# V of the memory rows turned by transposing DMA through DRAM in place of TensorE transposes

## The chip, the cores and the metric

The kernel runs on one core of a Trainium2 chip. The metric is device time in microseconds (us). A kernel's runs mostly lie within 0.2% of each other. The names in the profile: PE is TensorE's matmuls, PEld its weight loads, DVE is VectorE, ACT ScalarE, POOL GpSimd, and SP the engine whose queue issues most of the DMAs (SPq in the views).

## The reference, cut to what matters

Two independent heads are concatenated. Head A is a state-space layer; its last stage is a matmul that shares TensorE with the start of head B. Head B is attention over segments of 32 tokens, each with 8 memory rows in front; the memory is the output of the segment before:

```python
for s in range(n_seg):                       # 64 segments of 32 tokens, 32 heads of 128
    h = jnp.concatenate([mem, xs], axis=1)   # 8 memory rows + 32 tokens
    q, k, v = (jnp.einsum('btd,dhe->bhte', h, W) for W in (Wq, Wk, Wv))
    ...                                      # masked softmax
    o = jnp.einsum('bhqk,bhke->bhqe', p, v)
    o = jnp.einsum('bhte,hed->btd', o, Wo)
    mem = o[:, :M, :].copy()
```

The kernel guesses all memory rows at once (73 distinct rows), computes everything in parallel, and checks the guess at the end. The change concerns only V of those 73 rows.

## The kernel before: the parts that matter

`v_mem(hb)` computes V of the 73 memory rows for one block of four heads. There are eight blocks (`hb`). The product leaves PE with the head dimension on the partitions, so it must be turned before it goes to DRAM (`b_vx`, `b_vt`), from where the attention loads it together with V of the tokens.

```python
def v_mem(self, hb, w=None):
    p = k.ps("P")
    ...                                            # 32 matmuls: V transposed, 4 heads x 73 columns
    vm = self.vmp.tile([128, 4, NM], BF16, name="b_vm", bufs=1)
    k.copy("v", vm[:], ...p...)                    # DVE: PSUM to SBUF
    yield
    pt = k.ps("P", (128, 1024), BF16)
    for h in range(4):
        k.PE.transpose(pt[0:NM, h * 128:(h + 1) * 128], vm[:, h, :], k.ident[:])
    st = self.next_st()                            # one of two staging buffers b_vst, in turn
    k.copy("v", st[0:NM, 0, :, 0:E], ...pt...)     # DVE: PSUM to SBUF
    sv = st[:, 0, :, :].rearrange("p h e -> p (h e)")
    k.SP.dma_start(self.vx[hb][64:64 + NMX, :], sv[0:NMX, :])
    k.SP.dma_start(self.vt[hb][:], sv[NMX:NM, :])
    yield
```

Each row of V carries a column of ones (for the softmax sum); in the staging buffer these columns were set once, at the start. Blocks 0 and 1 are turned during the last output tiles of head A (`i` 26 to 29 of 32). Blocks 2 to 7 are turned inside the attention loop, two head pairs ahead of their use.

Right after blocks 0 and 1 the attention starts with its first load of V:

```python
def load_v(self, hp):
    ...
    if hp < 2:      # zeros for the partitions that V does not fill: 128 - GW = 29 of them
        z = self.vx[0][T + 32:T + 32 + 128 - GW, 0:2 * EW].unsqueeze(1).to_broadcast([128 - GW, NG, 2 * EW])
        k.tc.keep_in_program_order(k.SP.dma_start(vt[GW:128, :, :], z))
    ...             # then 96 partitions from b_vx, 3 from b_vt
```

Of the kernel before, what the change touches and what calls it, by code (L numbers as in the profile page):

```python
# [9 lines left out]
BF16 = mybir.dt.bfloat16  # L10
# [16 lines left out]
HB = 8; HP = 16  # L27
# [7 lines left out]
NMX = 7  # L35
NM = NTL + NMX
# [3 lines left out]
EW = E + 8  # L40
# [13 lines left out]
class Pinned:  # L54


    def __init__(self, k, name, eng):
        self.k, self.name, self.eng = k, name, eng
# [278 lines left out]
class PartB:  # L337
    def __init__(self, k, x, mem0, Wq, Wk, Wv, Wo, out):
        self.k = k
        self.x, self.mem0, self.out = x, mem0, out  # L340
        self.Wf = [w.rearrange("(c p) h e -> p c (h e)", p=128) for w in (Wq, Wk, Wv)]
        self.Wo = Wo.rearrange("h e d -> e h d")
        self.vx = [k.drp.tile([NSLOT, 4 * EW], BF16, name=f"b_vx{i}") for i in range(HB)]
        self.vt = [k.drp.tile([NTL, 4 * EW], BF16, name=f"b_vt{i}") for i in range(HB)]
        self.on = [k.drp.tile([T, 1024], BF16, name=f"b_on{i}") for i in range(4)]
        self.tn = [k.drp.tile([NR, 1024], BF16, name=f"b_tn{i}") for i in range(4)]
        c = k.cst
        self.m0T = c.tile([128, KC, M], BF16, name="b_m0T")
        self.gx = c.tile([128, KC, NM], BF16, name="b_gx")
        self.vmp = c  # L350
        self.xbar = c.tile([128, KC, NSEG], BF16, name="b_xbar")
        self.ogT = c.tile([128, H, NSEG], BF16, name="b_ogT")
        self.accE = c.tile([128, HP * NU], FP32, name="b_accE")
        self.accR = c.tile([128, HP * 2 * NG], FP32, name="b_accR")
        self.flag = c.tile([1, 1], I32, name="b_flag")
# [184 lines left out]
    def v_mem(self, hb, w=None):  # L540
        k = self.k
        w = w or self.load_wv(hb)
        p = k.ps("P")
        for h in range(4):
            for c in range(KC):
                k.PE.matmul(p[:, h * NM:(h + 1) * NM], w[:, c, h * 128:(h + 1) * 128], self.memT[:, c, :], start=(c == 0), stop=(c == KC - 1))
        vm = self.vmp.tile([128, 4, NM], BF16, name="b_vm", bufs=1)
        k.copy("v", vm[:], p[:, 0:4 * NM].rearrange("p (h n) -> p h n", h=4))
        yield
        pt = k.ps("P", (128, 1024), BF16)  # L550
        for h in range(4):
            k.PE.transpose(pt[0:NM, h * 128:(h + 1) * 128], vm[:, h, :], k.ident[:])
        st = self.next_st()
        k.copy("v", st[0:NM, 0, :, 0:E], pt[0:NM, 0:512].rearrange("p (h e) -> p h e", h=4))
        sv = st[:, 0, :, :].rearrange("p h e -> p (h e)")
        k.SP.dma_start(self.vx[hb][64:64 + NMX, :], sv[0:NMX, :])
        k.SP.dma_start(self.vt[hb][:], sv[NMX:NM, :])
        yield


# [414 lines left out]
def kernel_main(tc, A_x, A_Lre, A_Lim, A_Bre, A_Bim, A_Cre, A_Cim, A_logdt, A_Dskip, B_x, B_mem0, B_Wq, B_Wk, B_Wv, B_Wo, out,  # L975
                force=False, dbg=None):
    with ExitStack() as ctx:
        k = K(tc, ctx)
# [3 lines left out]
        b = PartB(k, B_x, B_mem0, B_Wq, B_Wk, B_Wv, B_Wo, out)  # L982

        def pool(name, side, bufs=2):
            return tc.tile_pool(name=name, bufs=bufs, side=side, reuse_waits="tile")
# [8 lines left out]
        with pool("p1x", "right") as p1x, pool("p1", "right", 1) as p1:  # L994
# [10 lines left out]
            wv = {0: w0, 1: b.load_wv(1)}  # L1005
# [17 lines left out]
            for kind, pc, q in order[1:]:  # L1023
# [3 lines left out]
                if kind == "v":  # L1027
                    b.v_x(pc, q, wv[pc])
                    if q == 3:
                        if pc >= 3:  # L1030
                            b.og(pc, wv[pc])
                        n = (pc + 2) if pc + 2 < PC else (2, 0)[pc + 2 - PC]
# [3 lines left out]
                n = 4 * pc + q  # L1036
# [27 lines left out]
        with pool("p2h", "right") as p2h, pool("p2", "right") as p2:  # L1064
            a.s2_tiles(p2h, p2)
            g = b.guess(p2)
            s2 = a.stage2()
            b.wog = []
            a.load_h(1, nc.scalar)
            for i, _ in enumerate(s2):  # L1070
                if i in (1, 4, 7):
                    n = (2, 0, 1)[(i - 1) // 3]
                    b.og(n, wv[n], "O")
                    if n == 2:
                        wv[1] = b.load_wv(1)
                if i in (3, 7, 11, 15):
                    b.load_wog((3, 7, 11, 15).index(i), p2)
                if i in (9, 11, 13, 15, 17, 19, 21, 22):
                    next(g)
                if i == 20:  # L1080
                    b.load_wqk(0)
                if i == 23:
                    for _ in g:
                        pass
                if i in (26, 28):
                    vm = b.v_mem((i - 26) // 2, wv[(i - 26) // 2])
                if 26 <= i < 30:
                    next(vm)


# [15 lines left out]
        for n, (hp, u) in enumerate(at):  # L1106
            if n == 12:
                k.SP.dma_start(wo0[:], b.Wo[:, :, 0:512])
            if hp % 2 == 0 and 2 < hp + 2 < HP:
                if u == 4:  # L1110
                    vm = b.v_mem(hp // 2 + 1)
                if u in (4, 6):
                    next(vm)
            if hp == 13 and u in (3, 6, 9):
                b.load_o_early(u // 3 - 1)
            want = min(18 * HP, LEAD + (n + 1) * 18 // 11)
            while done < want:
                next(pr)
                done += 1
            if done == 18 * HP:  # L1120
                if first is None:
                    xs.close()
                    b.p4a = ctx.enter_context(pool("p4a", "left", 1))
                    wo1 = b.p4a.tile([128, H, 512], BF16, name="wo1")
                    b.wo = (wo0, wo1)
                    b.load_o_early(3)
                    for h in range(0, H, 16):
                        k.SP.dma_start(wo1[:, h:h + 16, :], b.Wo[:, h:h + 16, 512:D])
                    first = b.outproj_first()
                next(first)  # L1130
# [30 lines left out]
@with_exitstack  # L1161
def kernel(
    ctx: ExitStack,
    tc: tile.TileContext,
    A_x: bass.AP,
    A_Lambda_re: bass.AP,
    A_Lambda_im: bass.AP,
    A_B_re: bass.AP,
    A_B_im: bass.AP,
    A_C_re: bass.AP,  # L1170
    A_C_im: bass.AP,
    A_log_dt: bass.AP,
    A_Dskip: bass.AP,
    B_x: bass.AP,
    B_mem0: bass.AP,
    B_Wq: bass.AP,
    B_Wk: bass.AP,
    B_Wv: bass.AP,
    B_Wo: bass.AP,
    B_seg_len: bass.AP,  # L1180
    out: bass.AP,
):
    assert int(B_seg_len) == SEG
    kernel_main(tc, A_x, A_Lambda_re, A_Lambda_im, A_B_re, A_B_im, A_C_re, A_C_im, A_log_dt, A_Dskip,
                B_x, B_mem0, B_Wq, B_Wk, B_Wv, B_Wo, out)
# [35 lines left out]
```

## Time and profile before

| kernel before | |
|---|---|
| time | 1247.24 us, median of 4 runs (1247.18 to 1247.70) |
| span of the profiled run | 1245.6 us |
| PE busy | 1234.4 us (99%) |

Three lines of the page of the kernel before (busy time, share of the span, number of instructions; then the chain of waits by engine):

```profile
span 1245.6 us, 20120 instructions
PE 1234.4 (99%) x8270; PEld 662.3 (53%) x8342; DVE 668.0 (54%) x1250; ACT 263.5 (21%) x631; POOL 275.8 (22%) x407
PE 98%; DMA 1%; issue 0%; ACT 0%; POOL 0%; DVE 0%; SPq 0%; ACTq 0%
```

PE is the bottleneck from end to end. Its own list of waits, whole (who waited for whom: us in total, times, longest), holds 2.4 us:

```profile
PE psR L64 <- DVE hpb L105: 1.3, 1, 1.3
PE psO L64 <- POOL b_m L644: 0.9, 3, 0.4
PE psP L64 <- ACT b_xe L89: 0.2, 1, 0.2
```

So whatever makes PE wait lengthens the kernel. PE's timeline of the kernel before shows the four transposes of block 0 between two runs of head A's matmuls, and later the first use of `b_v`. Columns: start, length, engine, line, operation, operands, count.

```profile
455.76 0.39 PE L64 MATMUL psP<-ident,b_vm 128*73 128x128 bf16 x4
455.99 3.62 PE L64 MATMUL psP<-t,a_hl 128*128 128x512 bf16 x16
...
492.05 0.34 PE L64 MATMUL psS<-b_q,b_k 128*128 128x99 bf16 x4
492.23 0.50 PE L64 MATMUL psO<-b_v,b_m 128*128 128x129 bf16 x6
```

Records of matmuls overlap, so the length of a row overstates its cost; from start to next start the four transposes hold PE for 0.23 us. SP's timeline of the kernel before around the same place (the length is how long SP is in the issue, not how long the data takes):

```profile
457.01 0.30 SPq L64 DMA_DIRECT2D b_vx<-b_vst  x1
457.36 0.30 SPq L64 DMA_DIRECT2D b_vt<-b_vst  x1
460.71 0.41 SPq L64 DMA_DIRECT2D b_wv<-in_B_Wv_dram  x1
465.22 0.27 SPq L64 DMA_DIRECT2D b_vx<-b_vst  x1
465.54 0.30 SPq L64 DMA_DIRECT2D b_vt<-b_vst  x1
465.93 0.25 SPq L64 DMA_DIRECT2D b_v<-b_vt  x1
466.23 16.11 SPq L64 DMA_DIRECT2D b_v<-b_vx  x2
```

The last line is the 29-partition zero fill and the main load. SP sits in them for 16 us, and PE uses the result at 492.23 without a wait. Narrower windows of the same view show the two apart:

```profile
466.23 0.32 SPq L64 DMA_DIRECT2D b_v<-b_vx  x1
466.60 15.74 SPq L64 DMA_DIRECT2D b_v<-b_vx  x1
```

By the semaphore updates in the trace, the last part of the main load landed at 491.56 us, 0.7 us before its use.

### The profile page before, as it was taken

The page shows a single profiled execution, that of the slowest core. Times are in us where ns is not written, and L with a number is a line of the kernel's source. Part 1 is how long each engine was busy: PE and PEld are TensorE (multiplying, and loading weights), DVE is VectorE, ACT ScalarE, POOL GpSimd, SP SyncE. Part 2 cuts the span into 40 slices and gives each one's busy share as a digit, 9 for nine tenths or more (in the row PEclk, how much of TensorE's full clock was granted, in tenths as well). Part 3 has the DMA queues.
Part 4 walks back from the last instruction along what each step waited for, and adds up shares of the span by engine and source line. Part 5 has one row for each costly group of instructions (what it writes and reads, how often), then busy time and mean ns, then how long its engine had stood idle before and what let it go on. Part 6 is the DMA issues. An engine that isn't in the chain of part 4 may idle for free.

```text
span 1245.6 us, 20120 instructions
## 1 busy us (share of the span) xinstructions
PE 1234.4 (99%) x8270; PEld 662.3 (53%) x8342; DVE 668.0 (54%) x1250; ACT 263.5 (21%) x631; POOL 275.8 (22%) x407
## 2 busy tenths in 40 slices
PE   9999999999999999999999999999999999999998
PEld 5444444444455555556666656555665554446444
DVE  4688899998711124666666666666666641001000
ACT  5344444443310000211112111111211110000000
POOL 4111331212332321322222222222222220000000
PEclk9999999999999999999999999999999999999999
DMA  9965444554898834664454544545473289407000
GB/s 245 272 192 148 131 132 128 144 156 107 241 323 247 251 116 95 192 167 123 95 144 108 144 108 114 138 92 133 96 155 95 61 223 220 110 18 153 17 17 27
DMA packets 316022, 176.83 MB, mean 142 GB/s; under 512 B 138650, under 2 KB 301326, under 8 KB 315926
## 3 DMA queue, kind: packets, MB, share of 16 engines
q1 hardware_dynamic: 293830, 147.95, 48.1%
q10 hardware_dynamic: 21072, 24.38, 5.9%
q0 software_dynamic: 1024, 3.17, 0.7%
q8 instruction: 66, 1.08, 0.4%
q14 instruction: 30, 0.25, 0.1%
HBM read 89.14 MB, written 53.17 MB: 114 GB/s over the span
## 4 chain that ended last, share of the span: by engine, by line
PE 98%; DMA 1%; issue 0%; ACT 0%; POOL 0%; DVE 0%; SPq 0%; ACTq 0%
PE psP L64 82%; PE psU L64 9%; PE psS L64 3%; PE psO L64 2%; PE psR L64 2%; DMA wo<-in_B_Wo_dram 1%; DMA b_xr<-in_B_x_dram 0%; ACT b_xe L89 0%; POOL b_m L644 0%; DVE b_ost L91 0%; SPq L64 0%; ACT b_e L641 0%; ACTq L89 0%
## 5 line engine op out<-in xcount | busy, mean ns | idle before, releaser
L64 PE MATMUL psP<-b_xe,b_wq 128*128 128x480 bf16 (+1 forms) x1280 | 247.7, 343 | 0.1
L64 PE MATMUL psP<-b_xe,b_wk 128*128 128x480 bf16 (+1 forms) x1280 | 247.7, 343 | 0.0
L64 PE MATMUL psP<-b_wv,b_xe 128*128 128x512 bf16 (+2 forms) x1033 | 223.4, 372 | 1.0 <-ACT b_xe L89 0.2
L644 POOL TENSOR_TENSOR b_m<-b_e,maskB 99x396 bf16<-99x396 bf16 x160 | 139.8, 874 | 334.0 <-ACT b_e L641 334.0
L641 ACT ACTIVATE b_e<-psS 99x396 bf16<-99x396 f32 x176 | 88.2, 501 | 532.2 <-PE psS L64 527.9
L64 PEld LDWEIGHTS <-b_wk 128*128 128x128 bf16 x1280 | 119.4, 98 | 94.2
L64 PEld LDWEIGHTS <-b_wq 128*128 128x128 bf16 x1280 | 118.7, 98 | 87.7
L64 PEld LDWEIGHTS <-b_xe 128*128 128x128 bf16 x1056 | 101.8, 98 | 119.1 <-ACT b_xe L89 0.4
L91 DVE CAST b_k<-psP 128x480 bf16<-128x480 f32 (+1 forms) x192 | 97.5, 529 | 101.1 <-PE psP L64 101.1
L91 DVE CAST b_q<-psP 128x480 bf16<-128x480 f32 (+1 forms) x192 | 97.5, 529 | 93.0 <-PE psP L64 91.4
L64 PEld LDWEIGHTS <-b_ol 128*128 128x128 bf16 x864 | 84.3, 98 | 94.4
L64 PE MATMUL psU<-a_xT,a_bt 128*128 128x512 bf16 x493 | 113.9, 379 | 1.1
L64 PE MATMUL psP<-t,a_hl 128*128 128x512 bf16 x496 | 112.1, 379 | 0.8
L91 DVE CAST b_ost<-psP 128x512 bf16<-128x512 f32 (+1 forms) x17 | 11.5, 676 | 183.4 <-PE psP L64 182.4
L64 PE MATMUL psP<-wo,b_ol 128*128 128x512 bf16 (+1 forms) x440 | 91.9, 364 | 0.4
L64 PE MATMUL psP<-t,b_ol 128*128 128x512 bf16 x408 | 91.7, 379 | 0.4
L280 POOL TENSOR_SCALAR a_tt<-a_pr,a_tabf 128x1 f32<-128x1 f32 x48 | 34.1, 709 | 243.5 <-DVE a_pr L275 243.5
L89 ACT ACTIVATE b_vst<-psP 128x512 bf16<-128x512 f32 x126 | 72.0, 589 | 71.0 <-PE psP L64 65.0
L661 DVE TENSOR_TENSOR b_ob<-psO,b_accR 99x384 bf16<-99x384 f32 x160 | 85.9, 553 | 2.0
L267 DVE TENSOR_TENSOR a_pr<-psU,a_tabf 128x2048 f32<-128x2048 f32 x32 | 73.0, 2282 | 15.7 <-PE psU L64 14.0
L64 PEld LDWEIGHTS <-a_bt 128*128 128x128 bf16 x512 | 49.2, 98 | 57.6
L64 PEld LDWEIGHTS <-a_hl 128*128 128x128 bf16 x512 | 49.1, 98 | 56.7
(200 smaller groups left out, 963.8 us busy)
## 6 DMA issues: line engine op xcount, KB each, us to landing
b_v<-b_vx SPq DMA_DIRECT2D x16, 1122.0 KB
b_wv<-in_B_Wv_dram SPq DMA_DIRECT2D x16, 1024.0 KB
b_on<-b_ob SPq DMA_DIRECT2D x15, 960.0 KB
b_vx<-b_vst ACTq DMA_DIRECT2D x24, 544.0 KB
a_hs<-a_h SPq DMA_DIRECT2D x32, 256.0 KB
b_wog<-in_B_Wo_dram SPq DMA_DIRECT2D x4, 2048.0 KB
b_wq<-in_B_Wq_dram SPq DMA_DIRECT2D x16, 512.0 KB
b_wk<-in_B_Wk_dram SPq DMA_DIRECT2D x16, 512.0 KB
```

The lines of the kernel that those rows point to most:

```text
L64: r = f(*a, **kw)
L89: self.S.activation(out, in_, ACT.Copy)
L91: self.V.tensor_copy(out, in_)
L267: V.tensor_tensor(pr[:], u[:].unsqueeze(1).to_broadcast([128, 2, 2, TB]), view(t3, [[TB + 1, 2], [TB + 1, 2], [1, TB]]), ALU.mult)
L280: G.tensor_scalar(tt[:, j:j + 1], w[:, j, TB - 1:TB], t3[:, 1, TB:TB + 1], None, ALU.mult)
L641: k.S.activation(e[:], s[0:GW, :, :, 0:GW], ACT.Exp, scale=float(E) ** -0.5, accum_out=self.accE[0:GW, i:i + 1])
L644: k.G.tensor_tensor(m[0:GW, 0:4 * GP].rearrange("p (a b q) -> p a b q", a=2, b=2)[:, :, :, 0:GW], e[:], mask[0:GW, :, :].unsqueeze(2).to_b ...
L661: V.tensor_tensor(self.ob[:, b0:b0 + n, :], o[0:GW, 0:n, 0:E], r.unsqueeze(2).to_broadcast([GW, n, E]), ALU.mult)
```

## The change

The intent is to take 32 transposes off PE and 8 copies off DVE. V of the memory rows is written to DRAM as it is (`b_vmt`), and a transposing DMA brings it back turned. The diff, cut to its core:

```diff
+        self.vmt = [k.drp.tile([4, E, 128], BF16, name=f"b_vmt{i}") for i in range(HB)]
...
-        vm = self.vmp.tile([128, 4, NM], BF16, name="b_vm", bufs=1)
-        k.copy("v", vm[:], p[:, 0:4 * NM].rearrange("p (h n) -> p h n", h=4))
+        ...                                # self.vm: one buffer of 128 columns per head, kept for all blocks
+        k.copy("v", self.vm[:, :, 0:NM], p[:, 0:4 * NM].rearrange("p (h n) -> p h n", h=4))
+        k.SP.dma_start(self.vmt[hb].rearrange("h e n -> e h n"), self.vm[:])
         yield
-        ...                                # four PE transposes, one DVE copy
+        s = self.next_st()[:].rearrange("p i h e -> p (i h e)")[:, 0:576].rearrange("p (h e) -> p h e", h=4)
+        k.V.memset(s[:, :, E:EW], 1.0)
         for h in range(4):
-            ...
+            k.SP.dma_start_transpose(s[:, h, 0:E], self.vmt[hb][h])
+        yield
+        k.SP.dma_start(self.vx[hb][64:64 + NMX, :].rearrange("n (h e) -> n h e", h=4), s[0:NMX, :, 0:EW])
+        k.SP.dma_start(self.vt[hb].rearrange("n (h e) -> n h e", h=4), s[NMX:NM, :, 0:EW])
         yield
```

Each block now takes three steps in place of two, so blocks 0 and 1 start at `i` 25 and 28 (before: 26 and 28), and the later blocks run at `u` 4, 6 and 8. The staging buffer has another row pitch, so its ones columns are set again for every block (the memset).

More of the change, by code (lines that the diff above doesn't have):

```diff
@@ L546, in v_mem @@
                 k.PE.matmul(p[:, h * NM:(h + 1) * NM], w[:, c, h * 128:(h + 1) * 128], self.memT[:, c, :], start=(c == 0), stop=(c == KC - 1))
-        vm = self.vmp.tile([128, 4, NM], BF16, name="b_vm", bufs=1)
-        k.copy("v", vm[:], p[:, 0:4 * NM].rearrange("p (h n) -> p h n", h=4))
+        if hb == 0:
+            self.vm = self.vmp.tile([128, 4, 128], BF16, name="b_vm", bufs=1)
+            k.V.memset(self.vm[:, :, NM:128], 0.0)
+        k.copy("v", self.vm[:, :, 0:NM], p[:, 0:4 * NM].rearrange("p (h n) -> p h n", h=4))
+        k.SP.dma_start(self.vmt[hb].rearrange("h e n -> e h n"), self.vm[:])
         yield
-        pt = k.ps("P", (128, 1024), BF16)
+        s = self.next_st()[:].rearrange("p i h e -> p (i h e)")[:, 0:576].rearrange("p (h e) -> p h e", h=4)
+        k.V.memset(s[:, :, E:EW], 1.0)
         for h in range(4):
-            k.PE.transpose(pt[0:NM, h * 128:(h + 1) * 128], vm[:, h, :], k.ident[:])
-        st = self.next_st()
-        k.copy("v", st[0:NM, 0, :, 0:E], pt[0:NM, 0:512].rearrange("p (h e) -> p h e", h=4))
-        sv = st[:, 0, :, :].rearrange("p h e -> p (h e)")
-        k.SP.dma_start(self.vx[hb][64:64 + NMX, :], sv[0:NMX, :])
-        k.SP.dma_start(self.vt[hb][:], sv[NMX:NM, :])
+            k.SP.dma_start_transpose(s[:, h, 0:E], self.vmt[hb][h])
+        yield
+        k.SP.dma_start(self.vx[hb][64:64 + NMX, :].rearrange("n (h e) -> n h e", h=4), s[0:NMX, :, 0:EW])
+        k.SP.dma_start(self.vt[hb].rearrange("n (h e) -> n h e", h=4), s[NMX:NM, :, 0:EW])
         yield
@@ L1084, in kernel_main @@
                         pass
-                if i in (26, 28):
-                    vm = b.v_mem((i - 26) // 2, wv[(i - 26) // 2])
-                if 26 <= i < 30:
+                if i in (25, 28):
+                    vm = b.v_mem((i - 25) // 3, wv[(i - 25) // 3])
+                if 25 <= i < 31:
                     next(vm)
@@ L1111, in kernel_main @@
                     vm = b.v_mem(hp // 2 + 1)
-                if u in (4, 6):
+                if u in (4, 6, 8):
                     next(vm)
```

## The prediction

> **What bounds the kernel.** TensorE. The page gives PE busy 1234.4 of 1245.6 us (99%), and the chain of waits is 98% PE. PE's own list of waits holds 2.4 us in all. So the change can gain only PE time, and can lose where a DMA arrives after PE wants it.
>
> **Removed.** 32 transposes, PE `psP<-ident,b_vm`, record 219 ns. The records overlap: in the timeline four of them hold PE from 455.76 to 455.99, so 0.23 us per head block. Eight blocks: 1.84 us, all on the critical path. Also 8 DVE copies of 394 ns (`b_vst<-psP` 73x512), off the path. PE's order is otherwise the same, but the first V product of the memory rows moves one step earlier.
>
> **Added, all in the SP queue:** per block a 131 KB write of V to DRAM, four 128x128 transposing DMAs that wait for it, and two stores that wait for those. SP issues in order.
>
> **Blocks 2 to 7** (in attention): the first stores leave SP at 572 us, the load of V that needs them at 593. 10 us more fit: no loss.
>
> **Blocks 0 and 1** (end of the state-space output stage) are tight. Before, SP stores block 1 at 465.2 to 465.8 and then issues the first loads of V (`b_v<-b_vt` 465.93, `b_v<-b_vx` from 466.23). The first of the latter is a 29-partition fill; SP sits in it for some 16 us, and DMA moves 22 to 30 GB/s in most slices: it goes through one engine (Trainium skill, "DMA: Bandwidth & Descriptors", section on why a DMA increments its semaphore by 16; the engines used must divide the partitions, so 29 gets one; the trace agrees). The big load follows, and that one engine's share ends at about 491. PE first uses `b_v` at 492.2. Slack: about 1 us.
>
> After: `b_wv` load (1 MB) still issued at about 460.5, when PE is done with that buffer; behind it the DRAM write, landing about 467; four transposes, landing about 470.5 (before, a 128x1024 one is issued in 1.3 to 1.5 us and its packets end about 2.5 us after issue); then two stores, then the V loads at about 472, 4.5 to 8 us late, say 6. The stall at the first `psO<-b_v` is then 6 minus 1 of slack plus 0.5 (PE arrives earlier), about 5 us, all paid: PE has no later idle time to win it back.
>
> Further, after a stall over 3.4 us TensorE may restart at half clock for up to 3.4 us (Trainium skill, "TensorE: Matmul & The Clock Gate", "Why this matters for your kernels"). The first eight 128x512 matmuls in this trace took 631 ns against 379 later, which agrees. I allow about 1 us for it.
>
> Sum: -1.84 + 5 (+1) = about +4. Predicted 1251.0 us, range 1246.5 to 1256.0. Chances: faster by over 2% 0.01, within 2% 0.97, slower by over 2% 0.02.
>
> **What would show it.** PE's list of waits: a new entry of about 5 us at `psO<-b_v`, on a DMA. SP's timeline: `b_v<-b_vx` starting near 472, not 466. PE busy lower by about 2 us (slow restart: 128x480 matmuls near 497 longer than their 366 ns). Blocks 2 to 7: SP gets waits on DMA, PE none.
>
> **What would make it wrong.** Small transposes slower (over 2 us each in series): 10 us and more lost. Or the DRAM write lands sooner and the fill starts within 2 us of before: then the 1.8 us gain remains, about 1245.5.

## The result

The changed kernel takes 1263.03 us (median of 4 runs, 1262.38 to 1264.79), the kernel before 1247.24. Ratios here and below are the mean time of one kernel's runs over that of the kernel before in the same rounds, so not quite the ratio of the medians quoted: 1.0128, 95% interval 1.0111 to 1.0146. The change makes the kernel 1.3% slower. The prediction had 1251 and at most 1256.

From the page of the changed kernel: its span, its busy times, and its chain by engine.

```profile
span 1260.7 us, 20102 instructions
PE 1236.5 (98%) x8240; PEld 661.4 (52%) x8310; DVE 666.4 (53%) x1251; ACT 263.6 (21%) x631; POOL 275.7 (22%) x407
PE 93%; DMA 5%; SPq 1%; issue 0%; DVE 0%; POOL 0%; ACT 0%; ACTq 0%; DVEq 0%
```

PE lost 30 of its recorded instructions (32 went), yet is busy 2.1 us longer. Its list of waits, but for two of 0.4 and 0.2 us for loads in the first 20 us:

```profile
PE psP L64 <- DVE b_q L91: 8.0, 1, 8.0
PE psO L64 <- DMA b_v<-b_vx: 4.7, 1, 4.7
PE psR L64 <- DVE hpb L105: 1.3, 1, 1.3
PE psO L64 <- POOL b_m L647: 0.9, 3, 0.4
PE psP L64 <- DVE b_vm L91: 0.8, 1, 0.8
```

The 4.7 us wait for `b_v` is the one predicted. The larger wait, 8.0 us on DVE, was not. PE's timeline of the changed kernel at the two waits:

```profile
474.85 1.78 PE L64 MATMUL psP<-b_xe,b_wq 128*128 128x480 bf16 x8
484.61 3.15 PE L64 MATMUL psP<-b_xe,b_wq 128*128 128x480 bf16 x8 [7.98 <-DVE b_q L91]
...
507.58 0.57 PE L64 MATMUL psO<-b_v,b_m 128*128 128x129 bf16 x6 [4.71 <-DMA b_v<-b_vx]
507.95 3.41 PE L64 MATMUL psP<-b_xe,b_wk 128*128 128x480 bf16 x8
```

Eight matmuls of the same form take 1.78 us before the first wait, 3.15 after it and 3.41 after the second. The table of stretches (start and end; busy us and instructions of each engine; then PEclk, the granted clock of TensorE; DMA share and GB/s) names the reason, for the clock is 0.57 and 0.59 there:

```profile
484.00:488.00 4.00, 3.39 (x10) 1.34 (x11) 2.28 (x13) 0.00 (x0) 0.00 (x0) 0.57 0.08 23
488.00:508.00 20.00, 15.29 (x90) 7.84 (x89) 6.83 (x16) 1.78 (x6) 2.62 (x3) 1.00 0.58 122
508.00:512.00 4.00, 4.00 (x20) 1.80 (x18) 1.83 (x6) 0.34 (x1) 0.00 (x0) 0.59 0.07 21
```

This fits the Trainium skill, page "TensorE: Matmul & The Clock Gate", Part 1, which states that TensorE runs at half clock after an idle window of about 3.4 us and needs as long to warm up again; a narrower window of the trace, 507.9 to 511.3 us, has a clock of 0.50 throughout.

The sum closes. Waits added: 8.0 + 4.7 + 0.8 + 0.4 = 13.9 us. Slow restarts: (3.15 - 1.78) + (3.41 - 1.78) = 3.0 us. Transposes removed: 8 x 0.23 = 1.8 us. Together +15.1 us; the spans differ by 1260.7 - 1245.6 = 15.1 us.

Now SP's timeline of the changed kernel, to be held against the seven lines shown of before:

```profile
450.00 0.63 SPq L64 DMA_DIRECT2D b_vmt<-b_vm  x1
...
455.62 4.98 SPq L64 DMA_TRANSPOSE b_vst<-b_vmt  x4
463.42 0.98 SPq L64 DMA_DIRECT2D b_vx<-b_vst  x1
464.44 0.85 SPq L64 DMA_DIRECT2D b_vt<-b_vst  x1
465.40 0.47 SPq L64 DMA_DIRECT2D b_wv<-in_B_Wv_dram  x1
468.60 0.39 SPq L64 DMA_DIRECT2D b_vmt<-b_vm  x1
472.81 4.96 SPq L64 DMA_TRANSPOSE b_vst<-b_vmt  x4
479.07 0.82 SPq L64 DMA_DIRECT2D b_vx<-b_vst  x1
479.94 0.83 SPq L64 DMA_DIRECT2D b_vt<-b_vst  x1
480.81 0.47 SPq L64 DMA_DIRECT2D b_v<-b_vt  x1
481.33 16.19 SPq L64 DMA_DIRECT2D b_v<-b_vx  x2
```

Four transposes keep SP for 5.0 us, 1.25 us each. Block 0's stores leave at 463.42 (457.01 before), the weights of a later block at 465.40 (460.71), block 1's stores at 479.07 (465.22), and the first big load of V starts 15.1 us later than before.

DVE's timeline of the changed kernel shows where the other wait comes from:

```profile
468.05 0.09 DVE L555 MEMSET b_vst<- 128x32 bf16 x1 [7.43 <-DMA b_vt<-b_vst]
468.11 0.47 DVE L91 CAST b_vm<-psP 128x292 bf16<-128x292 f32 x1
...
482.83 0.09 DVE L555 MEMSET b_vst<- 128x32 bf16 x1 [9.86 <-DMA b_vt<-b_vst]
```

Two memsets of 0.09 us each wait 7.43 and 9.86 us for a store to land, and what DVE does behind them waits too: the copy of block 1's V at 468.11, which PE's next buffer in PSUM (the memory that PE writes to) hangs on, and the copies of the first q and k. The instruction order of the built kernel says which memsets these are. Numbers in front are positions on DVE; `b_vst1` and `b_vst0` are the two staging buffers:

```
284 L555 Memset b_vst1_174  [waits ...]                      block 0
286 L555 Memset b_vst0_172  [waits ...]                      block 1
318 L91 TensorCopy b_vm_4414<-psP_4381                       block 0
322 L555 Memset b_vst1_174  [waits DMAHW6_49,DMAHW4_49]      block 2
323 L91 TensorCopy b_vm_4414<-psP_4489                       block 1
327 L555 Memset b_vst0_172  [waits DMAHW7_49,DMAHW6_49]      block 3
482 L91 TensorCopy b_vm_4414<-psP_5676                       block 2
```

(The last column is added here, shapes are cut.) The scheduler put the memsets of blocks 2 and 3, which nobody needs for another 100 us, in front of block 1's copy and of the attention's first copies. Each waits until the stores of block 0 or 1 have left the same buffer.

### The profile page after: what moved, and what is told of

Read it like the earlier page. It is cut to its first block, busy times and chain, and to the rows that moved or that the text cites. A ratio compares the mean times of both kernels' runs of the same rounds, so it can differ in the third digit from the quotient of the medians.

```text
span 1260.7 us, 20102 instructions
## 1 busy us (share of the span) xinstructions
PE 1236.5 (98%) x8240; PEld 661.4 (52%) x8310; DVE 666.4 (53%) x1251; ACT 263.6 (21%) x631; POOL 275.7 (22%) x407
## 4 chain that ended last, share of the span: by engine, by line
PE 93%; DMA 5%; SPq 1%; issue 0%; DVE 0%; POOL 0%; ACT 0%; ACTq 0%; DVEq 0%
PE psP L64 77%; PE psU L64 9%; PE psS L64 3%; PE psO L64 2%; DMA b_v<-b_vx 2%; PE psR L64 2%; SPq L64 1%; DMA b_vmt<-b_vm 1%; DMA wo<-in_B_Wo_dram 1%; DMA b_wv<-in_B_Wv_dram 1%; DMA b_vst<-b_vmt 0%; DMA b_vt<-b_vst 0%; DVE b_vm L91 0%; POOL b_m L647 0%; DVE b_ost L91 0%
```

## The experiments

Theory A: the added chain in the SP queue is too long ahead of the first load of V, because each small transpose costs 1.25 us of SP and block 0's part is not done when block 1's begins. It makes `b_v` late, and it also makes the two early memsets late, so the two waits of PE have one root and overlap. Rivals: the memset wait is a cost of its own that simply adds (Theory B); or the new traffic of blocks 2 to 7 costs something as well.

| run | edit | median us (lowest to highest) | ratio to before, 95% interval |
|---|---|---|---|
| changed kernel | | 1263.03 (1262.38 to 1264.79) | 1.0128 (1.0111 to 1.0146) |
| ones_once | memset for blocks 0 and 1 only | 1263.21 (1262.23 to 1265.99) | 1.0129 (1.0113 to 1.0144) |
| fill32 | fill over 32 partitions | 1257.41 (1257.29 to 1257.76) | 1.0080 (1.0065 to 1.0096) |
| ones_fill32 | both of these | 1246.22 (1245.48 to 1247.27) | 0.9993 (0.9979 to 1.0007) |
| tail_only | blocks 0, 1 on PE | 1245.90 (1245.76 to 1246.67) | 0.9989 (0.9975 to 1.0002) |
| one_transpose | one transposing DMA per block | 1255.61 (1254.25 to 1255.78) | 1.0067 (1.0051 to 1.0082) |
| all_three | ones once, fill32, one transpose | 1245.54 (1245.24 to 1246.01) | 0.9987 (0.9973 to 1.0000) |
| before_fill32 | kernel before with fill32 | 1246.93 (1246.87 to 1247.39) | 0.9997 (0.9984 to 1.0011) |
| defer1 | ones once, block 1 in attention | 1249.88 (1247.96 to 1249.94) | 1.0013 (0.9999 to 1.0027) |

All gave correct results. The kernel before measured 1247.49 (1247.03 to 1247.84) beside the second to fifth rows and 1247.29 (1247.00 to 1247.69) beside the last four.

### ones_once: take the memset's wait away

```diff
-        k.V.memset(s[:, :, E:EW], 1.0)
+        if hb < 2:
+            k.V.memset(s[:, :, E:EW], 1.0)
```

> Changed kernel, but the memset of the ones columns of the staging buffer runs only for blocks 0 and 1 (the columns stay valid afterwards), so DVE no longer waits for the stores of blocks 0 and 1. Theory A (two waits with one root, the late SP chain; they overlap): PE's 8.0 us wait on DVE b_q and the 0.8 us wait on b_vm go, but b_v still lands near 507 us, so PE waits there some 15 us instead of 4.7; one slow restart fewer: 1260 to 1262.5 us. Theory B (DVE's memset wait is a cost of its own): about 10 us faster, 1253 us.

The time did not move: 1263.21 us. Both waits on DVE are gone from PE's list, and the wait for `b_v` has grown to take their place:

```profile
PE psO L64 <- DMA b_v<-b_vx: 16.3, 1, 16.3
```

Theory B falls. PE came to `b_v` at about 492.7 us, as it does without the change, and waited until 509.0. The expected range was missed by 0.7 us; in the profiled run SP was 1.4 us later still (main load from 482.71 us, not 481.33). DVE's wait had cost nothing by itself: while it lasted, PE waited for DVE instead of waiting later, and longer, for the DMA.

### fill32: take the long fill away

```diff
-                z = self.vx[0][T + 32:T + 32 + 128 - GW, 0:2 * EW].unsqueeze(1).to_broadcast([128 - GW, NG, 2 * EW])
-                k.tc.keep_in_program_order(k.SP.dma_start(vt[GW:128, :, :], z))
+                z = self.vx[0][T + 32:T + 32 + 128 - GX, 0:2 * EW].unsqueeze(1).to_broadcast([128 - GX, NG, 2 * EW])
+                k.tc.keep_in_program_order(k.SP.dma_start(vt[GX:128, :, :], z))
...
-                k.SP.dma_start(wo0[:], b.Wo[:, :, 0:512])
+                k.tc.keep_in_program_order(k.SP.dma_start(wo0[:], b.Wo[:, :, 0:512]))
```

The second part keeps a 4 MB load where it was; without it the scheduler moved that load in front of the first load of V.

> Changed kernel, but the zero fill of the tail of b_v covers 32 partitions (96 to 127) and not 29, so that it can be spread over all DMA engines; the load of Wo stays pinned in its place. Theory A: SP is in the fill for 1 to 3 us and not 16, b_v lands near 491 us, before PE asks (502 us, held by DVE till then): the 4.7 us wait and its slow restart go, the 8.0 us wait on DVE stays: 1255 to 1257 us. If the single engine is not the reason, no change: 1263.

Fill and main load together now keep SP for 1.07 us in place of 16.19 (SP's timeline and PE's list of waits of this run):

```profile
481.64 1.07 SPq L64 DMA_DIRECT2D b_v<-b_vx  x2
```

```profile
PE psP L64 <- DVE b_q L91: 8.6, 1, 8.6
```

The wait for `b_v` is gone, the wait on DVE stays, and the time is 1257.41 us, 0.4 above the expected range (8.6 us of wait in place of 8.0, and 1.0 on `b_vm`). Three partitions more set SP free 15 us sooner. That agrees with the Trainium skill, "DMA: Bandwidth & Descriptors", "Why a DMA increments its semaphore by 16 and not by 1": a DMA issued from SP uses the largest number of engines up to 16 that divides both sides' slowest dimension, so 29 partitions go through one engine and 32 through 16. The semaphore updates in the traces agree: after the issue, one engine reports the fill done in the changed kernel (at 502.0 us), 16 in this run (from 485.3 to 487.2 us).

### ones_fill32: both

The edit is the two diffs above together.

> Both of the above together. Theory A: PE asks for b_v at about 491.5 us and it lands at 489 to 492: no wait or about 1 us, and what remains is the removed transposes, minus 1.8 us: 1245 to 1247 us. If another cost of the change exists (traffic in attention), it stays above 1248.

PE's list of waits has neither of the two any more, and the time is 1246.22 us. Alone, the first edit gave 0 us and the second 5.6; together they give 16.8. That is the mark of two waits that lie over each other, and Theory A's claim. Some runs reach only 1247.27, and the spread is wider than the kernel before's; that some of these runs wait a little for `b_v`, whose last part landed in the profiled one at 492.1 us and was used at 492.24, is likely but not shown.

### tail_only: where is the loss?

`v_mem` keeps the four PE transposes and the copy for `hb < 2` and takes the new path from block 2 on, with the ones set once per buffer:

```diff
+        if hb < 2:
+            ...            # the old path, word for word
+            return
         s = ...
-        k.V.memset(s[:, :, E:EW], 1.0)
+        if hb < 4:
+            k.V.memset(s[:, :, E:EW], 1.0)
```

> Blocks 0 and 1 turned by TensorE as before, blocks 2 to 7 by the transposing DMA (ones set once per buffer). If the whole loss lies in blocks 0 and 1 and the six later blocks cost nothing, each saves 0.23 us: 1.4 us faster than before, 1245.9 us. If the later blocks cost anything by traffic or by waits in the SP queue, 1247.2 us or more.

1245.90 us, as expected. Six of the eight blocks gain what the change was made for: all five runs lie below all nine of the kernel before, though the interval of the ratio just includes 1. The whole loss sits in blocks 0 and 1. In the changed kernel too, the attention shows no PE gap: from 560 to 960 us PE is busy 400.00 of 400 us before and after, with a DMA share of 0.50 before and 0.54 after.

### one_transpose: is it the number of transposes?

```diff
-        self.vmt = [k.drp.tile([4, E, 128], BF16, name=f"b_vmt{i}") for i in range(HB)]
+        self.vmt = [k.drp.tile([E, 4 * 128], BF16, name=f"b_vmt{i}") for i in range(HB)]
...
-        k.SP.dma_start(self.vmt[hb].rearrange("h e n -> e h n"), self.vm[:])
+        k.SP.dma_start(self.vmt[hb][:], self.vm[:].rearrange("p h n -> p (h n)"))
...
-        for h in range(4):
-            k.SP.dma_start_transpose(s[:, h, 0:E], self.vmt[hb][h])
+        k.SP.dma_start_transpose(s[:, :, 0:E], self.vmt[hb][:])
```

> Changed kernel with V kept in DRAM as rows of 4 x 128, so that one transposing DMA turns all four heads of a block in place of four, and the write is of 1024-byte rows. The memset and the 29-partition fill stay. Theory A: SP spends about 1.4 us per block on the transposes in place of 5.0; the V loads start 7 to 9 us earlier (near 473 us), b_v lands near 499; DVE's wait ends near 474 us, so PE's 8.0 us wait on DVE falls under 2 us; PE then waits about 7 us for b_v: 1253 to 1256 us.

SP's timeline, block 1 and the first loads:

```profile
468.20 1.23 SPq L64 DMA_TRANSPOSE b_vst<-b_vmt  x1
470.73 0.81 SPq L64 DMA_DIRECT2D b_vx<-b_vst  x1
...
473.00 16.49 SPq L64 DMA_DIRECT2D b_v<-b_vx  x2
```

One transposing DMA of four heads keeps SP for 1.23 us, as long as one of a single head did. The first loads start 8.3 us earlier than in the changed kernel, the wait on DVE falls from 8.0 to 0.8 us, and the one for `b_v` is 6.2 us. The time is 1255.61 us, as expected. With memset and fill untouched, about half of the loss is gone; this is the direct test that the length of the chain was the root. The edit also makes the rows of the write to DRAM longer, but this is not where the time went: from the write's issue to the first transpose it is 6.0 and 4.1 us for blocks 0 and 1, against 5.6 and 4.2 in the changed kernel.

### all_three and before_fill32

`all_three` combines the three edits. `before_fill32` is the control: the same edit of the fill in the kernel before.

> Ones set once, fill over 32 partitions, one transposing DMA per block. Theory A: no wait on PE is left that the kernel before has not; b_v lands 6 us or more before PE asks: minus 1.84 us, 1245 to 1246 us, with less spread than with two of the three edits, where b_v landed within 1 us of its use.

> Kernel before with the fill over 32 partitions (and the load of Wo pinned in its place). In it b_v landed within about 1 us of its use without holding PE, so Theory A says no gain: 1247.0 to 1247.6 us. If the fill cost the kernel before anything, it gets faster.

`all_three` measured 1245.54 us and is the fastest kernel here; the first `b_v` has landed by 483.8 us, 8 us before PE uses it. PE's list of waits, whole:

```profile
PE psR L64 <- DVE hpb L105: 1.3, 1, 1.3
PE psO L64 <- POOL b_m L647: 0.9, 3, 0.4
PE psP L64 <- DMA b_wv<-in_B_Wv_dram: 0.3, 1, 0.3
```

It is the list of the kernel before but for the third line, of 0.3 us. The gain of 1.75 us (1247.29 - 1245.54) is the 1.84 us of transposes to within the scatter. All its runs lie below all runs of the kernel before, but 0.14% is little and the interval ends at 1.0000. The control gained nothing that stands out (1246.93 against 1247.29 us): the slow fill had been hidden before. The change made it matter. Held against this control, which has the same fill, `all_three` gains 1.39 us; how much of the 1.84 us is really won is not resolved more finely than that.

### defer1: move block 1 out of the way instead

```diff
-                if i in (25, 28):
-                    vm = b.v_mem((i - 25) // 3, wv[(i - 25) // 3])
-                if 25 <= i < 31:
+                if i == 25:
+                    vm = b.v_mem(0, wv[0])
+                if 25 <= i < 28:
...
-            if hp % 2 == 0 and 2 < hp + 2 < HP:
+            if hp % 2 == 0 and hp + 2 < HP:
                 if u == 4:
-                    vm = b.v_mem(hp // 2 + 1)
+                    vm = b.v_mem(hp // 2 + 1, wv[1] if hp == 0 else None)
```

The ones are set once, as in `ones_once`.

> Changed kernel with ones set once and block 1 turned in the attention stage like blocks 2 to 7; four transposes per block and the 29-partition fill as in the change. Only block 0 is then ahead of the first V loads, whose first DMA starts at about 465.5 us, where it stood before. Theory A: no stall at b_v, 1245 to 1246.5 us. If the transposing DMA itself costs PE time by traffic, it stays above 1247.5.

This missed. The first loads of V left SP at 467.3 us, not 465.5 (the one of `b_vt` had to wait for block 0's store to land), PE came 0.7 us earlier than in the kernel before (491.5 against 492.2 us), and PE waited 2.4 us:

```profile
PE psO L64 <- DMA b_v<-b_vx: 2.4, 1, 2.4
```

The five runs fall into two groups: 1247.96 and 1248.04, and 1249.88, 1249.93 and 1249.94. The profiled run is of the slower group; in its table of stretches the granted clock is 0.50 for 3.4 us:

```profile
495.20:498.60 3.40, 3.40 (x16) 1.70 (x14) 1.74 (x4) 0.59 (x2) 0.77 (x1) 0.50 0.07 21
```

In the stretches next to it, 493.9 to 495.2 and 498.6 to 502.0 us, it is 1.00: half clock began 1.3 us after PE had resumed. 3.4 x (1 - 0.50) = 1.7 us is about the distance between the groups, and the mean granted clock is 1.000 in the two faster runs and 0.998 to 0.999 in the three slower ones. So here a slow stretch was very likely paid in some runs and not in others; only one run has a trace. The run still shows that one block ahead of the first load ends at 1248 to 1250 us, where two ended at 1263.

## Why the prediction was wrong

- **What bounds the kernel, and the gain of 1.84 us:** right. `all_three` gained 1.75 us (1.39 against `before_fill32`) and `tail_only`, with six of eight blocks, 1.6.
- **Blocks 2 to 7 cost nothing:** right, by `tail_only` and by PE's 400.00 of 400 us in attention.
- **A stall at the first `psO<-b_v`, for the 29-partition fill runs through one engine and the slack was about 1 us:** the place and the reason were right (`fill32`, `ones_once`; the slack was 0.7 us). That the wait came out at 4.7 us, close to the 5 predicted, is luck: the loads were 15.1 us late and not 6, and PE came later too because it had already stood 8.0 us for DVE. Without that, in `ones_once`, the same wait is 16.3 us.
- **The size of the delay was the step that failed.** The prediction said: "`b_wv` load (1 MB) still issued at about 460.5", "the DRAM write, landing about 467", "four transposes, landing about 470.5", "the V loads at about 472, 4.5 to 8 us late, say 6". Measured: 465.4, 472.7, 478.9 and 481.3, so 15.1 us late. One term was mis-sized, and it counts for both blocks: SP's time in the transposes. Its 3.5 us from the write's landing to theirs, less the 2.5 us that it gives a transpose to land, leave about 1 us for the three issues before the last, as if SP's time went with the size of the 128x1024 one; it is 1.25 us for each 128x128 one, 5.0 us per block. And block 0 was taken to be done before 460.5 us; with 5.0 us in its transposes it held SP until 465.3, so block 1's chain began late. `one_transpose` shows that this is most of it: with 1.2 us per block the loads left at 473.0, 1 us from the 472 predicted. The prediction's own list of what would make it wrong names slower transposes, but only from 2 us each.
- **A wait that was not predicted at all:** DVE behind the early memsets, 8.0 us of PE. The prediction speaks of the order on PE and SP but not on DVE, where the memsets of blocks 2 and 3 stand in front with their DMA waits. As `ones_once` shows, this mistake alone would not have changed the time, since PE would have stood at `b_v` instead.
- **The slow restart:** right in kind, allowed at 1 us; it came twice and took 3.0 us. (The 3.4 us that the prediction takes from the page on the clock gate stand in its Part 1; the section that it names says about 3 us.)

## What to carry to other kernels

On a bottleneck engine without idle time, work that is moved to DMA is free only if the whole new chain (write, transposes, stores, each waiting for the one before) fits ahead of the first reader; find the tightest reader and add up the chain from measured issue times, which for the transposes here were per DMA and not per byte (1.25 us for one head, 1.23 for four). Look at the built order of every engine that the change touches, also of idle ones: a 0.09 us memset that waits for a DMA stops all that stands behind it. If one of two overlapping waits is taken away and nothing happens, that doesn't clear it; test the pair.

## What the Trainium skill lacked or had wrong

- "VectorE: DVE Perf Modes", "The three transpose paths", gives 390 ns for a TensorE transpose of 128x128 and 1309 ns by DMA, and doesn't say from where to where. In this kernel the stream of matmuls hides most of the first (four of 73x128 hold PE for 0.23 us), and the second is not the time to landing: SP is in the issue for 1.25 us, and in the chain of waits of the changed kernel it is 3.8 us (block 0) and 2.3 us (block 1) from the start of the last of four issues until its data have landed.
- No page says that SP's time in a transposing DMA is the same for one head as for four (1.25 us for 128x128, 1.23 us for 128x512); "DMA: Bandwidth & Descriptors" has a sequencer time per small transposing DMA only in its part on trn3, for earlier chips that it doesn't name. The advice of the same page, "Rules for kernel authors", to join small transfers agrees with it.
- By the same page's rule 29 partitions use one engine, but it doesn't say that the next issue is held behind such a DMA: the fill's own issue took 0.32 us, that of the load behind it 15.74 us, with all DMAs of SP behind it.
- "TensorE: Matmul & The Clock Gate" puts the idle time that halves the clock at about 3.4 us. In `defer1` a wait of 2.4 us was followed, 1.3 us after PE had resumed, by a granted clock of 0.50 for 3.4 us in the profiled run, and the times lie in two groups 1.9 us apart.
